# A cosFormer attention feeding a squared-ReLU MLP: the hand-written order of one Trainium2 core replaced by a list scheduler

## The chip, the cores and the metric

The kernel runs on one core of one Trainium2 chip. The metric is the device time of one launch in microseconds (us). A profile is one execution taken by the hardware profiler; its span runs from the first to the last instruction.

## The reference

There are 8 batches of 8 heads, 576 positions and a head width of 64. An attention without softmax comes first, then an MLP on all 4608 tokens:

```python
q_p = phi(q, cos_w, sin_w)      # relu(x)*cos, relu(x)*sin side by side: 128 features
k_p = phi(k, cos_w, sin_w)
kv = einsum('bhsf,bhsd->bhfd', k_p, v);  z = sum(k_p, axis=2)
x = einsum('bhsf,bhfd->bhsd', q_p, kv) / (einsum('bhsf,bhf->bhs', q_p, z) + 1e-06)
h = x.reshape(4608, 512) @ w_in          # 512 x 2048
out = relu(h)**2 @ w_out                 # 2048 x 512
```

Inputs and output are float32; the products are taken in bf16 and summed in float32.

## The kernel before

**Tiling.** Each batch's 576 positions are four tiles of 128 (j = 0 to 3) and a tail of 64 (j = 4). The attention of a batch is: features of k and q (cos half and sin half, L175 to L193), a cast of v into a tile that has a column of ones (L205), 40 small matmuls that give kv and z in one PSUM tile (`kz`, L246), its copy `kvz` (L257), the transposed features of q (by TensorE, L292, for batches 0 and 1; by a DMA transpose on SyncE's queue, L275, after that), eight matmuls of 65 columns per tile (`num`, L318), the division (three VectorE instructions, L328 to L332), and a transpose of x (TensorE L359 or DMA L350).

**First matmul** (`gemm1`, L391). A batch's 512 main tokens are two halves of 256. A slot is four of the 16 column blocks of w_in by 256 tokens: 16 matmuls of 256 columns into a two-bank PSUM tile, one ReLU of 128x1024 by ScalarE (L399), one square by VectorE (L406). The tails of two batches together are two more slots of 32 matmuls of 128 columns.

**Second matmul.** Batch 0 (L440) and one pair of tiles of batch 1 (L464) are plain, 512 columns wide. Everything else goes by pairs of 128-token tiles with Strassen's method in Winograd's form (`pair_mm`, L549): seven products (L533, eight matmuls of 256 columns each) from sums of blocks of g (`gs`, L529) and of w_out (`w2t`, L514). The products are added up by VectorE (L545) with two ScalarE copies (L569, L584), and the rows are stored from GpSimd's queue (L418).

**Order.** `slots` lists gemm1 and gemm2 slots of batch after batch; `at` and `plan` (L634 to L717) hang the attention pieces of later batches on slots by hand. All instructions of an engine run in the order in which they are issued. Loads of batches 0 to 3 are issued from GpSimd's queue, later ones from SyncE's (L709). Tiles of k, v, q and their tails have two buffers each (L62, L72). Before the slots come 31 matmuls on zeros (`warm`, L752), and batch 0's attention is written out (L771 to L790).

**PSUM.** Three pools: `hps` two tiles of two banks, `yps` two of one bank, `pa` one of two banks.

Of the kernel before, what the change touches and what calls it, by code (L numbers as in the profile page):

```python
# [15 lines left out]
FP = 512  # L16


@with_exitstack
def kernel(  # L20
# [15 lines left out]
    T = B * S  # L36
# [6 lines left out]
    assert P == 128 and H * D == 512 and D == 64 and TAIL == 64  # L43
# [4 lines left out]
    inp = ctx.enter_context(tc.tile_pool(name="inp", bufs=2))  # L48
    att = ctx.enter_context(tc.tile_pool(name="att", bufs=1))
    mlp = ctx.enter_context(tc.tile_pool(name="mlp", bufs=2))  # L50
    ps_h = ctx.enter_context(tc.tile_pool(name="ps_h", bufs=2, space=bass.MemoryType.PSUM))
    ps_y = ctx.enter_context(tc.tile_pool(name="ps_y", bufs=2, space=bass.MemoryType.PSUM))
    ps_a = ctx.enter_context(tc.tile_pool(name="ps_a", bufs=1, space=bass.MemoryType.PSUM))

    kqv = {}

    def load_main(src, nm, b, eng, parts=1):
        main = inp.tile([P, H, J, D], F32, name=nm, tag=nm, bufs=2)  # L62
        for i in range(parts):
            js = slice(i * J // parts, (i + 1) * J // parts)
            eng.dma_start(
                out=main[:, :, js, :],
                in_=src[b, :, 0:MAIN, :].rearrange("h (p j) d -> p h j d", j=J)[:, :, js, :],
            )
        kqv[nm, b] = main

    def load_tail(src, nm, b, eng):
        tail = inp.tile([P, HH, D], F32, name=nm + "t", tag=nm + "t", bufs=2)  # L72
        for g in range(2):
            eng.dma_start(
                out=tail[g * TAIL : (g + 1) * TAIL, :, :],
                in_=src[b, g * HH : (g + 1) * HH, MAIN:S, :].rearrange("h p d -> p h d"),
            )
        kqv[nm + "t", b] = tail

    def load_batch(b, eng, order):  # L80
        for nm in order:
            for part in (load_main, load_tail):
                part({"k": k, "v": v, "q": q}[nm], nm, b, eng)
# [3 lines left out]

# [28 lines left out]

# [17 lines left out]

    vexts = []
    for i in range(2):
        vx = att.tile([P, J, H, E1], BF16, name=f"vext{i}")
        vxt = att.tile([P, HH, E1], BF16, name=f"vextt{i}")
        for t in (vx, vxt):
            ones = t[:, :, :, D:E1] if t is vx else t[:, :, D:E1]  # L140
            nc.vector.memset(ones, 1.0)
        vexts.append((vx, vxt))
    kps, kvzs, kzs, qps, tqs, qpTs, xs = {}, {}, {}, {}, {}, {}, {}
    nums, xts, xtails = {}, {}, {}

    def cached(tiles, key, shape, tag, bufs):
        if key not in tiles:
            tiles[key] = att.tile(shape, BF16, name=tag, tag=tag, bufs=bufs)
        return tiles[key]


    def kp_of(b, j):
        if j == J:
            return cached(kps, (b, 1), [P, HH, F], "kpt", 1)
        return cached(kps, (b, 0), [P, J, H, F], "kp", 1)[:, j]

    def qp_of(b, j):
        if j == J:
            return cached(qps, (b, 2), [P, HH, F], "qpt", 2)
        return cached(qps, (b, j // 2), [P, 2, H, F], "qp", 2)[:, j % 2]  # L160

    def x_of(b, j):

        if j == J:
            return cached(xs, (b, 2), [P, 2, P], "xt", 2)
        return cached(xs, (b, j // 2), [P, KB, 2, P], "x", 2)[:, :, j % 2, :]

    def xT_of(b, i):
        return cached(xts, (b, i), [P, KB, 2 * P], "xT", 3)

    def xT_tails(m):

        return cached(xtails, m, [P, 2, 2, 2, TAIL], "xTt", 2)

    def feat_cos(dst, src, j):  # L175
        nc.vector.tensor_scalar(  # L176
            out=dst[:, :, 0:D],
            in0=src,
            scalar1=0.0,
            scalar2=cos_col[:, j : j + 1],  # L180
            op0=ALU.max,
            op1=ALU.mult,
        )

    def feat_sin(dst, src, j):
        nc.scalar.activation(  # L186
            out=dst[:, :, D:F], in_=src, func=ACTF.Relu, scale=sin_col[:, j : j + 1]
        )

    def feat_cos_act(dst, src, j):  # L190
        nc.scalar.activation(
            out=dst[:, :, 0:D], in_=src, func=ACTF.Relu, scale=cos_col[:, j : j + 1]
        )  # L193

    def att_k(b, j, cos=feat_cos):
        for f in (cos, feat_sin):
            f(kp_of(b, j), piece("k", b, j), j)

    def att_v(b, j, eng, h0=0, h1=H):
        copy = eng.copy if eng is nc.scalar else eng.tensor_copy  # L200
        vx, vxt = vexts[b % 2]
        if j == J:
            copy(out=vxt[:, :, 0:D], in_=piece("v", b, j))
        else:
            copy(out=vx[:, j, h0:h1, 0:D], in_=piece("v", b, j)[:, h0:h1, :])  # L205

    def warm(n):

        wm = ps_h.tile([P, 2, FP], F32, name="wm", tag="hps", bufs=2)
        for i in range(n):  # L210
            nc.tensor.matmul(
                out=wm[:, i % 2, :], lhsT=zeros[:, 0:P], rhs=zeros[:, :], start=True, stop=True
            )

    def fill(n):

        wm = ps_a.tile([P, 2, FP], F32, name="wm", tag="pa", bufs=1)
        for i in range(n):
            nc.tensor.matmul(
                out=wm[:, i % 2, :],  # L220
                lhsT=ident[:, :],
# [5 lines left out]
    def att_kv(b, part):  # L227
        vx, vxt = vexts[b % 2]
        if part == 0:
            kvzs[b] = att.tile([P, H, E1], BF16, name="kvz", tag="kvz", bufs=2)  # L230
            kzs[b] = ps_a.tile([P, 2, FP], F32, name="kz", tag="pa", bufs=1)
        kz = kzs[b]

        for j in (0, 1) if part == 0 else range(2, NS):
            for hh in range(HH):
                for half in range(2):
# [3 lines left out]
                    else:  # L243
# [3 lines left out]
                        out=kz[:, half, hh * E1 : (hh + 1) * E1],  # L247
# [5 lines left out]
        if part == 1 and b:  # L253
            att_kvz(b, nc.scalar.copy)

    def att_kvz(b, copy):
        copy(  # L257
            out=kvzs[b].rearrange("p (a h) e -> p a (h e)", a=2),
            in_=kzs[b][:, :, 0 : HH * E1],
        )  # L260

    def att_feat(b, j, parts="cs"):
        for c in parts:
            f = feat_cos if c == "c" else feat_sin
            f(qp_of(b, j), piece("q", b, j), j)

    def att_qT(b, i):

        n = 2 if i < J // 2 else 1
        nh = H if n == 2 else HH  # L270
        t = att.tile([P, n * nh, P], BF16, name="qpT", tag=f"qpT{n}", bufs=2)
        qp_of(b, 2 * i)
        src = qps[b, i]
        src = src.rearrange("p r h f -> p (r h f)") if n == 2 else src.rearrange("p h f -> p (h f)")
        nc.sync.dma_start_transpose(out=t[:, :, :], in_=src)  # L275
        for r in range(n):
            qpTs[b, 2 * i + r] = [
                t[:, r * nh + k * HH : r * nh + (k + 1) * HH, :] for k in range(nh // HH)
            ]

    def att_qT_pe(b, j, apart=False):

        nh = H if j < J else HH
        tq = ps_y.tile([P, H, P], BF16, name="tq", tag="yps", bufs=2)
        tqs[b, j] = [tq[:, 0:HH, :]]
        if apart:
            hi = ps_h.tile([P, HH, P], BF16, name="tqh", tag="hps", bufs=2)
            tqs[b, j].append(hi)
        elif nh == H:
            tqs[b, j].append(tq[:, HH:H, :])  # L290
        for h in range(nh):
            nc.tensor.transpose(  # L292
                tqs[b, j][h // HH][:, h % HH, :], qp_of(b, j)[:, h, :], ident[:, :]
            )

    def att_qT_copy(b, j, both=False):
        qpTs[b, j] = []
        for i, tq in enumerate(tqs[b, j]):
            t = att.tile([P, HH, P], BF16, name=f"qpTp{i}", tag=f"qpTp{i}", bufs=3)
            copy = nc.scalar.copy if both and i else nc.vector.tensor_copy  # L300
            copy(out=t[:, :, :], in_=tq[:, :, :])
            qpTs[b, j].append(t)

    def att_num(b, j, early=False):
        qpT, kvz = qpTs[b, j], kvzs[b]
        if early:
            num = ps_h.tile([P, 2, FP], F32, name="num", tag="hps", bufs=2)
        else:
            num = ps_a.tile([P, 2, FP], F32, name="num", tag="pa", bufs=1)
        for hh in range(HH):  # L310
            for half in range(2):
                e0 = hh * E1
                if j < J:
                    out, lhsT = num[:, half, e0 : e0 + E1], qpT[half][:, hh, :]
                else:
                    p0, p1 = half * TAIL, (half + 1) * TAIL
                    out, lhsT = num[p0:p1, 0, e0 : e0 + E1], qpT[0][:, hh, p0:p1]
                nc.tensor.matmul(  # L318
                    out=out, lhsT=lhsT, rhs=kvz[:, half * HH + hh, :], start=True, stop=True
                )  # L320
        nums[b, j] = num

    def att_div(b, j):
        n = 2 if j < J else 1
        n4 = nums[b, j][:, 0:n, 0 : HH * E1].rearrange("p b (h e) -> p b h e", e=E1)
        den = att.tile([P, 2, HH], F32, name="den", tag="den", bufs=2)
        rden = att.tile([P, 2, HH], F32, name="rden", tag="rden", bufs=2)
        nc.vector.tensor_single_scalar(  # L328
            out=den[:, 0:n], in_=n4[:, :, :, D], scalar=EPS, op=ALU.add
        )  # L330
        nc.vector.reciprocal(out=rden[:, 0:n], in_=den[:, 0:n])
        nc.vector.tensor_tensor(  # L332
            out=x_of(b, j).rearrange("p (b k) (l d) -> p b k l d", b=n, l=2),
            in0=n4[:, :, :, 0:D].rearrange("p b (k l) d -> p b k l d", l=2),
            in1=rden[:, 0:n]
            .rearrange("p b (k l) -> p b k l", l=2)
            .unsqueeze(4)
# [140 lines left out]

# [333 lines left out]
```

## Time and profile before

| what | us |
|---|---|
| time, median of 3 runs | 287.91 (287.77 to 288.2) |
| span of the profiled execution | 286.5 |
| TensorE (PE) busy, share | 279.0 (97%) |
| its weight loads (PEld) | 235.6 (82%) |
| VectorE (DVE) busy | 204.2 (71%) |
| ScalarE (ACT) busy | 161.8 (56%) |
| GpSimd (POOL) busy | 45.7 (16%) |
| moved by DMA | 53.04 MB, mean 185 GB/s |

The profiled execution's own time is not listed apart; its span stands 1.41 us below the median. A busy PE says that it never waits long, and not that each matmul takes what its columns need. Matmuls overlap, so their rate is read from the distance between starts in the chain of work or the timeline, not from a matmul's own duration. PEq, SPq and POOLq are the engines' own instruction queues.

### The profile page before, as it was taken

To read this page: it belongs to the slowest core of one execution; us is meant where nothing else is said; L and a number is where in the kernel's file an instruction comes from. 1 tells how busy PE (TensorE), PEld (TensorE's weight loads), DVE (VectorE), ACT (ScalarE), POOL (GpSimd) and SP (SyncE) were. 2 spreads that over 40 slices of the span, in tenths; PEclk is the share of its full clock that TensorE was granted. 3 is DMA by queue.
4 is the path that set the end of the run, shared out by engine and by line. 5 is a ranking of instruction groups with operands and counts; after the bars stand their busy time and mean duration, and the time that the engine had idled before them with its cause. 6 is when DMAs were issued, how large, how long until landed. Compare 5 with 4: busy or idle time off the path is not lost.

```text
span 286.5 us, 7327 instructions
## 1 busy us (share of the span) xinstructions
PE 279.0 (97%) x3067; PEld 235.6 (82%) x3067; DVE 204.2 (71%) x457; ACT 161.8 (56%) x245; POOL 45.7 (16%) x75
## 2 busy tenths in 40 slices
PE   8899999999999999999999999999999999999995
PEld 3578855888678888889988988888988888889884
DVE  1857664688697599787598776977677877547585
ACT  3764833679669669445881458844695461155210
POOL 8925507640000000000002000000000000000002
PEclk9999999999999999999999999999999999999999
DMA  7999996999457898999439975499809620300015
GB/s 236 298 206 302 329 263 197 362 364 277 57 119 187 212 275 195 237 301 212 136 106 192 348 160 165 107 267 287 227 9 237 114 46 3 140 9 2 0 76 146
DMA packets 73825, 53.04 MB, mean 185 GB/s; under 512 B 50496, under 2 KB 68416, under 8 KB 73792
## 3 DMA queue, kind: packets, MB, share of 16 engines
q1 hardware_dynamic: 63248, 26.75, 40.4%
q0 software_dynamic: 10400, 25.69, 29.8%
q8 instruction: 24, 0.39, 0.6%
q10 hardware_dynamic: 144, 0.13, 0.1%
q14 instruction: 9, 0.07, 0.1%
HBM read 36.70 MB, written 9.44 MB: 161 GB/s over the span
## 4 chain that ended last, share of the span: by engine, by line
PE 86%; DMA 5%; POOL 3%; DVE 2%; ACT 2%; issue 1%; POOLq 0%; ACTq 0%
PE hps L391 40%; PE ya L533 9%; PE yc L533 9%; PE yu L533 7%; DMA w1sb<-in_moe_w_in_dram 5%; PE yv L533 5%; PE num L318 3%; PE kz L246 3%; PE yps L464 2%; PE yps L440 2%; PE yh L440 2%; DVE ysb L545 1%; PE tq L292 1%; POOL w1sb L122 1%; DVE u L545 1%
## 5 line engine op out<-in xcount | busy, mean ns | idle before, releaser
L391 PEld LDWEIGHTS <-w1sb 128*128 128x128 bf16 x1344 | 113.4, 98 | 13.3 <-issue 2.0
L391 PE MATMUL hps<-xT,w1sb 128*128 128x256 bf16 (+1 forms) x1088 | 119.3, 266 | 1.2 <-DMA w1sb<-in_moe_w_in_dram 0.4
L399 ACT ACTIVATE rt<-hps 128x1024 bf16<-128x1024 f32 x72 | 73.7, 1023 | 68.1 <-PE hps L391 46.7
L406 DVE TENSOR_TENSOR gT<-rt 128x1024 bf16<-128x1024 bf16 x64 | 44.0, 687 | 20.1 <-ACT rt L399 20.1
L533 PEld LDWEIGHTS <-gs 128*128 128x128 bf16 x480 | 46.9, 98 | 5.4
L418 POOL DMA_DIRECT2D out_dram<-ysb x14 | 7.6, 541 | 171.6 <-DVE ysb L545 144.9
L533 PEld LDWEIGHTS <-gT 128*128 128x128 bf16 x312 | 29.8, 98 | 3.4
L332 DVE TENSOR_TENSOR x<-num,rden 128x512 bf16<-128x512 f32 x32 | 22.1, 692 | 1.1
L186 ACT ACTIVATE kp<-k,sin_col 128x512 bf16<-128x512 f32 x32 | 22.4, 717 | 0.6 <-DMA k<-in_k_dram 0.6
L186 ACT ACTIVATE qp<-q,sin_col 128x512 bf16<-128x512 f32 x32 | 22.0, 719 | 1.1 <-DMA q<-in_q_dram 1.1
L328 DVE TENSOR_SCALAR den<-num 128x8 f32<-128x8 f32 (+1 forms) x40 | 6.6, 164 | 20.6 <-PE num L318 20.4
L529 DVE TENSOR_TENSOR gs<-gT 128x1024 bf16<-128x1024 bf16 x26 | 17.8, 684 | 0.0
L533 PE MATMUL ya<-w2t,gs 128*128 128x256 bf16 x120 | 15.6, 273 | 0.0
L533 PE MATMUL yc<-w2sb,gs 128*128 128x256 bf16 x120 | 15.6, 273 | 0.0
L533 PE MATMUL yu<-w2t,gs 128*128 128x256 bf16 x120 | 15.6, 272 | 0.0
L391 PE MATMUL hps<-xTt,w1sb 128*128 128x128 bf16 x256 | 15.1, 219 | 0.2 <-ACT rt L399 0.2
L176 DVE TENSOR_SCALAR qp<-q,cos_col 128x512 bf16<-128x512 f32 x32 | 14.7, 487 | 0.0
L533 PE MATMUL yu<-w2sb,gs 128*128 128x256 bf16 x112 | 14.5, 273 | 0.0
L205 ACT CAST vext<-v 128x512 bf16<-128x512 f32 x23 | 14.1, 614 | 0.6 <-DMA v<-in_v_dram 0.6
L584 ACT COPY s<-yu 128x256 f32<-128x256 f32 x14 | 5.2, 372 | 15.6 <-PE yu L533 15.6
L176 DVE TENSOR_SCALAR kp<-k,cos_col 128x512 bf16<-128x512 f32 x21 | 10.1, 504 | 5.0 <-DMA k<-in_k_dram 5.0
L533 PE MATMUL yc<-w2sb,gT 128*128 128x256 bf16 x104 | 13.5, 273 | 0.0
(98 smaller groups left out, 340.8 us busy)
## 6 DMA issues: line engine op xcount, KB each, us to landing
out_dram<-ysb POOLq DMA_DIRECT2D x14, 512.0 KB, 4.1
k<-in_k_dram SPq DMA_DIRECT2D x5, 1024.0 KB, 7.9
v<-in_v_dram POOLq DMA_DIRECT2D x4, 1024.0 KB, 8.6
v<-in_v_dram SPq DMA_DIRECT2D x4, 1024.0 KB, 8.7
q<-in_q_dram SPq DMA_DIRECT2D x4, 1024.0 KB, 6.7
q<-in_q_dram POOLq DMA_DIRECT2D x3, 1024.0 KB, 12.7
k<-in_k_dram POOLq DMA_DIRECT2D x3, 1024.0 KB, 10.0
w1sb<-in_moe_w_in_dram POOLq DMA_DIRECT2D x4, 512.0 KB, 11.2
```

The costliest lines, as they stand in the source:

```text
L176: nc.vector.tensor_scalar(out=dst[:, :, 0:D], in0=src, scalar1=0.0, scalar2=cos_col[:, j : j + 1], op0=ALU.max, op1=ALU.mult,)
L186: nc.scalar.activation(out=dst[:, :, D:F], in_=src, func=ACTF.Relu, scale=sin_col[:, j : j + 1])
L205: copy(out=vx[:, j, h0:h1, 0:D], in_=piece("v", b, j)[:, h0:h1, :])
L246: nc.tensor.matmul(out=kz[:, half, hh * E1 : (hh + 1) * E1], lhsT=lhsT, rhs=rhs, start=(j == 0 and hh == 0), stop=(j == J and hh == HH - 1),)
L318: nc.tensor.matmul(out=out, lhsT=lhsT, rhs=kvz[:, half * HH + hh, :], start=True, stop=True)
L332: nc.vector.tensor_tensor(out=x_of(b, j).rearrange("p (b k) (l d) -> p b k l d", b=n, l=2), in0=n4[:, :, :, 0:D].rearrange("p b (k l) d -> ...
L391: nc.tensor.matmul(out=out, lhsT=w1sb[:, kb, hb * P : (hb + 1) * P], rhs=rhs, start=(kb == 0), stop=(kb == KB - 1),)
L399: nc.scalar.activation(out=rt[:, :, :], in_=hps[:, :, :], func=ACTF.Relu)
L406: nc.vector.tensor_tensor(out=dst, in0=rt[:, :, :], in1=rt[:, :, :], op=ALU.mult)
L440: nc.tensor.matmul(out=ypss[b][tt], lhsT=gTs[b][:, hb, tt * P : (tt + 1) * P], rhs=w2sb[:, hb, :], start=(hb == 0), stop=(hb == HB - 1),)
L529: nc.vector.tensor_tensor(out=t[:, :, :], in0=in0, in1=in1, op=op)
L533: nc.tensor.matmul(out=acc, lhsT=lhs[:, hb, :], rhs=rhs[:, hb, :], start=(hb == 0), stop=(hb == HB2 - 1),)
```

## The change

The kernel's order is no longer written by hand. A class `Plan` takes every step with its engine, an estimated duration, the keys it reads and writes, and a due time; a greedy pass puts at each moment the ready step with the earliest due time on the engine that is free first, and the steps are then issued in that order. What is issued by hand as before: the loads of batch 0, of w_in, of batch 1 and of w_out, and batch 0's attention up to x of its first two tiles.

```diff
+class Plan:
+    LAG = {"PE": 0.24, "ACT": 0.1, "DVE": 0.1, "POOL": 0.1, "SP": 0.1}
+    def add(self, eng, dur, fn, r=(), w=(), due=None, size=0.0, lag=None, name="", after=0.0):
...
+        at = max([self.given.get(key, 0.0) for key in (*r, *w)] + [after])
...
+    def order(self, t0, rate, fixed):
...
+        free = {"PE": t0, "ACT": t0, "DVE": t0, "POOL": t0, "SP": t0, "DMA": t0}
...
+            i = min((i for i in waiting[e] if ready[i] <= s + 0.02), key=lambda i: (due[i], i))
...
+            if size:
+                free["DMA"] = max(free["DMA"], end) + size / rate
+                end = free["DMA"] + fixed
...
+    T0 = 16.8
...
+    plan.given.update({("v", j): 41.0 for j in range(J)})
+    plan.given.update({("kt", 0): 37.0, ("vt", 0): 42.0, ("qt", 1): 31.5, ("qt", 0): 26.0})
...
+        plan.run(T0, 0.38, 2.0)
```

Loads have one buffer per input (two for the tails of q), and all loads of batches 2 to 7 are steps of the plan on GpSimd's queue:

```diff
-        main = inp.tile([P, H, J, D], F32, name=nm, tag=nm, bufs=2)
+        main = home(inp, [P, H, J, D], nm, dtype=F32)
...
+    TAILS = {"k": 1, "v": 1, "q": 2}
...
+    def plan_load(b, nm, due, eng="POOL"):
+        size = 1.05
+        add(eng, 0.95, lambda: load_main(nm, b, ENG[eng]), w=[(nm, j) for j in range(J)], due=due, size=size)
```

The first matmul of batches 1 to 7 runs over all 512 main tokens at once; the tails of the eight batches (8 x 64 = 512 tokens) are a ninth batch. PSUM is six single banks and one double one (`abank`, for `kz` and `num`); a unit is four matmuls of 512 columns into bank 2, 0 or 1, with its own ReLU of 128x512; four units share one square of 128x2048. Batch 0 keeps its two halves.

```diff
+    def unit_mm(m, hb, to):
...
+        for kb in range(KB):
+            nc.tensor.matmul(
+                out=out_,
+                lhsT=w1sb[:, kb, hb * P : (hb + 1) * P],
+                rhs=x_block(m, kb),
+                start=(kb == 0),
+                stop=(kb == KB - 1),
+            )
```

The second matmul: batch 0 is plain as before; batches 1 to 8 each have seven products of two halves (eight matmuls of 256 columns each) over blocks of 256 tokens. Sums of products are kept in PSUM: where a sum goes on in another bank, ScalarE copies the bank (a seed), and later products are added on top by the matmuls.

```diff
+    YA, YB, YC = 3, 4, 5
...
+        prod(1)
+        seed(YA, YB)
+        prod(2)
+        last(YA, 0, 0, False)
+        prod(5)
+        add("ACT", cost("ACT", 512, "psum"), lambda: nc.scalar.copy(out=five_of(m)[:, :, :], in_=half_bank(YC)),
+            r=[("bank", YC)], w=[("five",)])
+        prod(6)
+        seed(YB, YC)
+        prod(7)
+        prod(3)
+        last(YB, 0, 1, True)
+        store(0)
+        last(YC, 1, 1, True)
+        prod(4)
+        last(YC, 1, 0, False)
+        store(1)
```

`last` is a ScalarE copy to the output tile, or with the flag a VectorE addition of product 5. Stores are issued from SyncE's queue; the ninth batch's are two groups of four of 64 rows. All cos features are made by VectorE and all sin features by ScalarE.

The built order of the changed kernel, engine by engine, has these places that the prediction speaks of. GpSimd: the four w_out loads end the part by hand, then `qt` of batch 2 (two tails), `q`, `k`, and later `v` of batch 2. ScalarE: sin features of batch 1's k and its tail, sin of batch 2's q tail, sin of batch 1's q tail, casts of v of batch 1 (tiles 2, 3, tail), four sin features of batch 2's q, copy `kvz` of batch 1. VectorE: cos of batch 1's k, square, cos of batch 2's q tail, cos of batch 1's q tail, casts of v of batch 1 (tiles 0, 1). TensorE: transposed q features of batch 1's tiles 2 and 3, the second matmul of batch 0 (16 steps of four matmuls), and in it, after the fifth step, `kz` of batch 1 in three parts, `num` and the transposes of x of batch 1.

## The prediction

> **What bounds the kernel now.** I read the page's busy times first, then the chain of work in order of time, then the timeline of the first 50 us. PE is busy 279.0 of 286.5 us, and the chain is PE nearly throughout, so every us is either a matmul's columns or a wait of PE.
>
> ```profile
> PE 279.0 (97%) x3067; PEld 235.6 (82%) x3067; DVE 204.2 (71%) x457; ACT 161.8 (56%) x245; POOL 45.7 (16%) x75
> PEclk9999999999999999999999999999999999999999
> ```
>
> The chain's stretches give PE's rates (start, us, what):
>
> ```profile
> 77.31 1.73 PE yps L464 x8
> ...
> 81.25 0.87 PE ya L533 x8
> ...
> 128.81 8.92 PE hps L391 x112
> ...
> 143.85 0.49 PE kz L246 x16
> ```
>
> 512 columns cost 1.73/8 = 216 ns and 256 columns 109 ns; the 112 are 48 wide ones (48 x 0.1092 = 5.24) and 64 of 128 columns, so (8.92 - 5.24)/64 = 57.5 ns; a 65-column one costs 0.030. Wide matmuls are hardly cheaper per column (216 against 2 x 109), so the change can save little on PE; the question is its waits. Where they come from is in the timeline (start, us, engine, line, what, idle before it):
>
> ```profile
> 16.79 1.96 PE L391 MATMUL hps<-xT,w1sb 128*128 128x128 bf16 x32
> ...
> 33.87 0.75 POOL L129 DMA_DIRECT2D w2sb<-in_moe_w_out_dram  x1 [2.48 <-DMA k<-in_k_dram]
> ...
> 34.61 0.91 POOL L65 DMA_DIRECT2D q<-in_q_dram  x1
> ...
> 39.15 1.44 DVE L205 CAST vext<-v 128x512 bf16<-128x512 f32 x4 [0.81 <-DMA v<-in_v_dram]
> ...
> 42.21 1.13 PE L246 MATMUL kz<-vext,kp 128*128 128x65 bf16 x32
> ```
>
> The reader is to see that loads arrive late here: GpSimd issues the last w_out load at 33.87 because it waits for one of the transfers under way, v of batch 1 lands only at 39.15, and PE comes to `kz` after that, at 42.21. DMA is full to 44 us. A small load on this queue stands behind the large ones (issues between 30 and 50 us, KB each, us to landing; the q tails of that answer were issued at 44.9, when the queue had drained):
>
> ```profile
> vt<-in_v_dram POOLq DMA_DIRECT2D x3, 64.0 KB, 7.7
> qt<-in_q_dram POOLq DMA_DIRECT2D x2, 64.0 KB, 2.4
> ```
>
> **The sum on PE.** After the first real matmul at 16.79, before has 960 of 256 and 384 of 128 columns in the first product (104.8 + 22.0), 96 of 512 and 840 of 256 in the second (20.8 + 91.7), 584 small ones (17.6) and 84 transposes (4.8): 261.7. After has 512 of 512, 96 of 256 and 64 of 128 (110.7 + 10.5 + 3.7), 64 of 512 and 896 of 256 (13.8 + 97.8), the same 584, and 72 transposes (4.1): 258.3. **Minus 3.4 us**: 1.7 of it from tails at 512 columns, the rest from widths and transposes. Before's last matmul ends at 283.09 (282.05 + 1.04), so 283.09 - 16.79 - 261.7 = 4.6 us are waits: 1.9 up to the first Strassen product at 81.25 (its place in the sum is 62.6 after the start), 2.7 after it.
>
> **Up to 16.79** nothing changes: the loads and batch 0's attention are issued as before. The q load of batch 1 has now to wait for the features of batch 0's q (the last cos ends at 17.04; it was issued at 12.71), but it stands behind w_in, whose last quarter is waited for at 24.43; I take no loss, at most the 4.3 us by which it is issued later.
>
> **16.8 to 36.5: +1.1.** w_in's third and fourth quarters are waited for as before (0.3 and 0.4). All four q tiles of batch 1 are transposed before the second matmul starts, not three. The fourth needs ScalarE's sin, which stands behind the two ReLUs of the last half slot: that slot ends near 34.4, two times 0.59 and 0.72 later it is 35.9. The second matmul starts at 36.5; by the sum it would be 35.4 (before: 34.9, then 0.5 lost at 35.94).
>
> **The main wait: +3.9.** In the built order both VectorE and ScalarE have a feature of batch 2's q tail ahead of the v casts of batch 1. That tail load is issued after the last w_out load, so not before 34.6, behind v and three quarters of w_out; with 7.7 us for such a load it lands at 42.3, and since q, issued at 34.61, lands with the draining of the queue near 45, I take 43.0 (ends: 37.0, by the 2.4 of an empty queue, and 45.3). The two tails (0.35 each) and two casts (0.42 each) make 44.65 before `kz` can start; PE is there, 4.3 us after 36.5, at 40.8. PE runs in order, so all later work slips. Then ScalarE has four sin features of batch 2's q (4 x 0.72 from 46.0, when that q lands) ahead of the `kvz` copy (0.59): `num` waits **+1.1**. At the end of this stage `num` of tile 3 is followed directly by the transposes of its x: a copy of 0.69 on VectorE and the division (0.17 + 0.20 + 0.69) stand between: **+1.8** with the smaller waits. In before these stretches had other work between them.
>
> **Steady state: waits as before, 2.7, and 1.5 on the way in.** ScalarE gains work: 144 ReLUs at 0.59 (row of a 128x512 PSUM copy, 586 ns) for 72 at 1.02 are +10.5, and 40 PSUM copies at 0.59 for 29 at 0.37 are +12.9, so about 185 us. A window of 28.5 us (one first and one second product) has 16 x 0.59 + 5 x 0.59 + 8 x 0.72 + 2 x 0.50 + 1.6 + 0.6 = 21.4 on it. VectorE loses about 25 (additions of products 42 to 11, +5 cos, small ones). Both stay below PE; that hides them, and a ReLU has two units (1.7 us) until its bank is wanted. A seed from PSUM to PSUM is in no row: between 0.37 (128x256) and 0.69 (VectorE, 128x512 float32); I take 0.59, nearest in shape. In the first such window VectorE has the eight sums of w_out (5.5) besides, and three features (0.5 + 0.4 + 0.7) stand ahead of the first seed: +1.5. Below these, 0; above, x's transposes: their DMA lands a median 4.0 after its issue and is wanted about 9 us after the last `num` of a batch, behind a transpose of q (3.9): it may cost 1 us in each of four windows.
>
> **The end: +1.6 and +1.9.** The ninth batch's products have no first matmul beside them. The first waits for ReLU and square (2.2 after the last unit against 1.75 of products: 0.5), product 7 for the seed (0.2 + 0.6 + 0.1, nothing else ready), product 4 for 0.1. After the last matmul come a ScalarE copy (0.59 for 0.42) and, on one queue, the rest of eight stores of 64 rows, about 0.55 apart: 3 x 0.55 more than before. 3.4 us (286.5 - 283.1) become 5.3.
>
> **Sum.** 44.65, plus the rest of the stream (258.3 less 22.2 up to `kz`: 236.1), plus 1.1 + 1.8 + 1.5 + 2.7 + 1.6, plus 5.3: a span of 294.7. The median stands 1.41 above the span: **296.1 us**, 2.9% slower.
>
> **A rule that would make it longer.** At the start the 31 matmuls on zeros take 8.46 us where 31 x 0.216 would be 6.7, so a cold PE lost 1.75 though the page grants it full clock. The Trainium skill, "TensorE: Matmul & The Clock Gate", section "Part 1: The HAM clock gate", says that PE falls to half clock after an idle window of some 3.4 us and needs as much busy time to recover. No wait of before is long enough to show it. If PE's wait at `kz` (3.9 us) sets this off, the price by the row is 1.75 again.
>
> **Rivals.** (1) The tail load lands at 45.3 (+2.3), or the wait slows PE (+1.75), or both: 297.8 to 300.1. For: DMA at its limit to 44 us. (2) The tail load lands before the casts are due (37.0): their chain then starts at 39.15, `kz` is hardly late, and 3.9 is not paid: 292.2; with 1.1 and 1.8 gone as well, 289.3. Against: the 7.7 us row. (3) Transposes or single-buffered loads arrive late in each window: 4 us more, 300.1. (4) Faster: the price is PE's own waits. If the new order removes the 1.9 and 2.7 of before and adds only the end's 3.5 less the sum's 3.4, it is 287.9 + 0.1 - 4.6 = 283.4; it turns faster once all of PE's waits ahead of the end stay below 4.5 us. For: no engine but PE is full in steady state. Against: the in-order queues above. That the change does not do what it says (waits elsewhere unchanged, PE sum unmoved) would give 287.9 + 3.5 = 291.4; I count it with (2).
>
> **Chances.** Forecast (293 to 297.5) 0.45; (1) 0.17; (2) 0.17; (3) 0.09; (4) 0.09; between (2) and no change 0.03. Range: from 288.5 to 300.5, which leaves out (4) and the far end of (3). A difference under 0.2% (0.6 us) can't be told from none: faster 0.09, same 0.03, slower 0.88.
>
> **What would show it.** Right: a gap of PE of some 4 us before `kz` of batch 1 near 41 to 45, with VectorE and ScalarE idle on a q-tail load before it; PE's sum near 258 after 16.8; a gap near 1 us before product 7 at the end and over 5 us after the last matmul. Wrong: the v casts at 39; PE gaps in each window; a second matmul that starts at 35; or a PE rate other than 216 ns.

## The result, and the profile after

The changed kernel takes **334.08 us** (median of 4 runs, 333.01 to 338.89) against 288.06 (287.77 to 289.03): a ratio of **1.159, 95% interval 1.154 to 1.163**. One of the four runs, the one of 338.89, counts as slow and is not in the ratio. The forecast of 296.1 had the sign right and missed the size by 38 us, and the time lies far above the range. The profiled execution has a span of 331.2 us, 36.5 over the forecast's 294.7.

The page of the changed kernel, with the rows that answer to those shown of before, and the shares of the chain of work:

```profile
PE 286.7 (87%) x2403; PEld 187.3 (57%) x2407; DVE 183.8 (55%) x368; ACT 173.6 (52%) x305; POOL 60.1 (18%) x89
...
PEclk9999979966999996898967999999999999999998
...
PE 58%; DMA 32%; DVE 3%; ACT 2%; issue 2%; POOL 1%; ACTq 0%; POOLq 0%; DVEq 0%
```

PE is 58% of the chain where it was 86% before; a third is DMA now, and the granted clock dips several times. The clock row's digits are the 40th parts of the span, 8.3 us each: all dips but the last digit lie in the first 22, before 183 us. The table by stage says the same in us (window; its length; PE, PEld, DVE, ACT, POOL busy; granted clock; DMA share; GB/s). Before:

```profile
16.00:60.00 44.00, 43.31 (x474) 32.71 (x472) 27.31 (x65) 23.53 (x34) 20.36 (x28) 1.00 1.05 284
60.00:120.00 60.00, 59.50 (x710) 49.98 (x709) 49.11 (x116) 45.14 (x73) 3.34 (x6) 1.00 0.84 206
120.00:180.00 60.00, 59.90 (x676) 53.80 (x674) 45.31 (x98) 36.13 (x54) 3.77 (x7) 1.00 0.76 200
```

After:

```profile
16.00:60.00 44.00, 36.42 (x372) 25.81 (x374) 25.62 (x59) 26.55 (x48) 22.24 (x30) 0.96 1.15 284
60.00:120.00 60.00, 49.09 (x432) 29.07 (x431) 44.37 (x95) 38.45 (x71) 14.73 (x21) 0.91 0.97 214
120.00:180.00 60.00, 43.95 (x339) 26.57 (x338) 28.64 (x59) 27.99 (x52) 8.86 (x13) 0.83 1.15 196
180.00:330.00 150.00, 143.44 (x1153) 98.43 (x1151) 76.26 (x128) 71.06 (x122) 2.97 (x5) 1.00 0.30 80
```

From 16 to 180 us PE stands 34.5 us idle (7.6 + 10.9 + 16.0) where before it stood 1.3, and part of its busy time ran at less than full clock. After 180 us, when nearly all loads are in, PE is busy almost throughout, at clock 1.00. So the new order can run without waits; something before 180 us prevents it, and the DMA engines are fuller there (0.97 and 1.15 against 0.84 and 0.76) though they move hardly more bytes per us (214 and 196 GB/s against 206 and 200). What PE's neighbours wait for (waiting instruction and what ended the wait; us in total, times, longest):

```profile
DVE qp L270 <- DMA qpT<-qp: 25.7, 3, 12.6
...
ACT qp L268 <- DMA qpT<-qp: 20.6, 4, 9.0
```

A feature of the next batch's q (L268, L270) overwrites the tile that the query transpose (L333, a DMA on SP) still reads. VectorE and ScalarE run in order, so ReLUs and squares behind it wait too, and PE behind those. The two largest waits of PE before 80 us, in its timeline:

```profile
46.23 1.04 PE L311 MATMUL abank<-vext,kp 128*128 128x65 bf16 x16 [5.86 <-DVE vext L288]
...
63.10 2.75 PE L435 MATMUL bank<-xT,w1sb 128*128 128x512 bf16 x12
74.75 1.86 PE L435 MATMUL bank<-xT,w1sb 128*128 128x512 bf16 x4 [8.89 <-ACT rt L448]
```

The first is the wait at `kz` that the prediction named. The second it did not have, and SP's own timeline shows its cause:

```profile
48.91 22.53 SPq L333 DMA_TRANSPOSE qpT<-qp  x2
```

Two transposes hold SP for 22.5 us, while POOL's queue has four 1 MB loads of batches 2 and 3 under way (issued from 47.62 to 57.67). Later waits of PE behind transposes are 7.6 us (to 130.9, for a transpose of x, which stands on SP's queue among those of q), 3.0 (to 146.3) and 3.3 (to 169.0) behind query transposes, and 1.2 for x again. Over the whole run the query transposes land a median 8.4 us after their issue, where before it was 3.9; those of x land after 4.3 (before: 4.0). In the kernel before, loads of batches 4 to 7 stood in one row with the transposes on SP; now all loads but the first are on POOL's queue, beside them.

### The profile page after: what moved, and what is told of

It reads as the page before. It is cut to its first block, busy times and chain, and to the rows that moved or that the text cites. A ratio compares the mean times of both kernels' runs of the same rounds, so it can differ in the third digit from the quotient of the medians.

```text
span 331.2 us, 6047 instructions
## 1 busy us (share of the span) xinstructions
PE 286.7 (87%) x2403; PEld 187.3 (57%) x2407; DVE 183.8 (55%) x368; ACT 173.6 (52%) x305; POOL 60.1 (18%) x89
## 3 DMA queue, kind: packets, MB, share of 16 engines
q1 hardware_dynamic: 48272, 21.50, 36.5%
q0 software_dynamic: 12032, 31.46, 34.5%
## 4 chain that ended last, share of the span: by engine, by line
PE 58%; DMA 32%; DVE 3%; ACT 2%; issue 2%; POOL 1%; ACTq 0%; POOLq 0%; DVEq 0%
PE bank L435 29%; PE bank L587 24%; DMA qpT<-qp 17%; DMA q<-in_q_dram 5%; DMA v<-in_v_dram 4%; DMA k<-in_k_dram 3%; DMA qt<-in_q_dram 2%; PE abank L364 2%; PE abank L311 1%; DMA xT<-x 1%; DVE x L384 1%; DVE kp L270 1%; ACT rt L448 0%; ACT qp L268 0%; PE bank L292 0%
## 5 line engine op out<-in xcount | busy, mean ns | idle before, releaser
L435 PE MATMUL bank<-xT,w1sb 128*128 128x512 bf16 x512 | 132.7, 395 | 20.6 <-ACT rt L448 11.9
L448 ACT ACTIVATE rt<-bank 128x512 bf16<-128x512 f32 x128 | 75.9, 597 | 76.3 <-PE bank L435 76.0
L435 PEld LDWEIGHTS <-w1sb 128*128 128x128 bf16 x512 | 49.5, 101 | 66.4 <-issue 21.1
L460 DVE TENSOR_TENSOR gT<-rt 128x2048 bf16<-128x2048 bf16 x32 | 39.1, 1222 | 44.4 <-ACT rt L448 44.3
L587 PEld LDWEIGHTS <-gT 128*128 128x128 bf16 x512 | 49.8, 99 | 20.5 <-DVE gT L460 3.6
L587 PE MATMUL bank<-w2sb,gT 128*128 128x256 bf16 x384 | 51.3, 277 | 4.7 <-DVE gT L460 3.3
L587 PE MATMUL bank<-w2t,gs 128*128 128x256 bf16 x256 | 34.0, 277 | 0.0
L268 ACT ACTIVATE qp<-q,sin_col 128x512 bf16<-128x512 f32 x32 | 21.8, 714 | 21.7 <-DMA qpT<-qp 20.6
L270 DVE TENSOR_SCALAR qp<-q,cos_col 128x512 bf16<-128x512 f32 x32 | 14.9, 510 | 31.5 <-DMA qpT<-qp 25.7
L268 ACT ACTIVATE kp<-k,sin_col 128x512 bf16<-128x512 f32 x32 | 21.3, 715 | 1.7 <-PE abank L311 1.1
L384 DVE TENSOR_TENSOR x<-abank,rden 128x512 bf16<-128x512 f32 x31 | 21.4, 691 | 1.1
L270 DVE TENSOR_SCALAR kp<-k,cos_col 128x512 bf16<-128x512 f32 x32 | 14.8, 506 | 9.0 <-DMA k<-in_k_dram 5.8
L780 ACT COPY ysb<-bank 128x512 f32<-128x512 f32 x16 | 9.4, 585 | 16.7 <-PE bank L587 16.5
L776 DVE TENSOR_TENSOR ysb<-bank,y 128x512 f32<-128x512 f32 x16 | 11.0, 688 | 12.8 <-issue 7.7
L587 PE MATMUL bank<-w2sb,gs 128*128 128x256 bf16 x128 | 16.6, 273 | 0.0
L587 PE MATMUL bank<-w2t,gT 128*128 128x256 bf16 x128 | 16.3, 273 | 0.0
```

The source lines that it names most:

```text
L268: eng.activation(out=dst[:, :, lo : lo + D], in_=src, func=ACTF.Relu, scale=col)
L270: eng.tensor_scalar(out=dst[:, :, lo : lo + D], in0=src, scalar1=0.0, scalar2=col, op0=ALU.max, op1=ALU.mult,)
L384: nc.vector.tensor_tensor(out=x[:, a:z], in0=n4[:, :, :, 0:D].rearrange("p b (k l) d -> p b k l d", l=2), in1=rden[:, a:z] .rearrange("p b ...
L435: nc.tensor.matmul(out=out_, lhsT=w1sb[:, kb, hb * P : (hb + 1) * P], rhs=x_block(m, kb), start=(kb == 0), stop=(kb == KB - 1),)
L448: eng.activation(out=rt_of(m, u)[:, i, :], in_=bank[to][:, :], func=ACTF.Relu)
L460: nc.vector.tensor_tensor(out=dst, in0=rt, in1=rt, op=ALU.mult)
```

## The experiments

**Theory A**: a query transpose that shares the DMA engines with loads of another queue takes several times as long, and the in-order engines carry this to PE. **B**: the planned order itself, with its single buffers, makes the waits. **C**: the falling clock is most of it. A fourth reading came with the first runs: the DMA is simply too full before 180 us, from whatever queue. The times below are single runs beside one or more of the kernel before (287.6 to 288.7) unless an interval is given; four runs of one version (e14) spread over 2.4 us, so a difference of 1 or 2 us between single runs settles nothing. The first number is the time, the span is that of the profiled execution.

**e1.** In `att_qT` the main transposes are left out; what reads them finds zeros.

```diff
-        nc.sync.dma_start_transpose(out=t[:, :, :], in_=src)
+        if n == 1:
+            nc.sync.dma_start_transpose(out=t[:, :, :], in_=src)
```

> Leaves out the twelve main transposes of the query features (SP, L333, batches 2 to 7); the numerators of these batches read a tile filled with zeros once at the start, and every other instruction and its order stay. Theory A (a transpose that shares the DMA engines with loads from POOL's queue takes 8 to 17 us instead of 2, and the features of the next batch, in order ahead of the ReLUs, wait for it): the waits of PE around 63, 123, 146 and 165 us shrink to under 2 us each (8.9 + 7.6 + 4 + 4.2 of idle, some 5 us of slow clock behind them), the wait at 46.2 stays, span 298 to 304 against 331.2. Theory B (the planned order itself: features and casts of later batches ahead of the ReLUs, single input buffers, a load queue blocked at its head; the transposes only happen to end last): other waits take their place, span above 315. Theory C (the falling clock is the larger part and follows any wait): the first wait alone costs most, span above 318.

299.97 us, span **297.8**. The wait at `kz` stays (4.7 us), and behind it PE waits at most 1.4 us at a time, as the windows show:

```profile
60.00:120.00 60.00, 57.78 (x533) 35.69 (x532) 53.93 (x115) 46.64 (x86) 17.99 (x25) 1.00 0.77 217
120.00:180.00 60.00, 60.00 (x536) 40.78 (x535) 41.62 (x84) 41.80 (x76) 9.77 (x14) 1.00 0.75 174
```

B and C in their strong forms fall: order and first wait are unchanged, and 33.4 us are gone with twelve transposes.

**e2.** `for i in range(parts if b < 4 else 0)` in `load_main`.

> Leaves out the twelve 1 MB loads of batches 4 to 7 (their features are made from the inputs of batch 3 again); the small loads of the tails, all transposes and the order stay. Theory A: the waits before 90 us stay (those loads are of batches 2 and 3), those at 123, 146 and 165 go, 7.6 + 4 + 4.2 us and some 4 of slow clock: span 308 to 314; each transpose of the queries after 90 us issues in 2 to 3 us. Rival (the transposes are slow by themselves, or through the stores and the small loads beside them): they still take 5 to 12 us and the span stays above 325.

314.54 us, span 312.6, within theory A's range. After 87 us the query transposes issue in 1.7 to 3.0 us and PE has no wait of 1 us or more; the wait before 80 us is there, and longer (13.5). So a transpose is not slow by itself: it needs the loads beside it.

**e3, e4.** `plan_load(b, nm, None, "POOL" if b < 4 else "SP")`, and `"SP"` for all.

> The loads of batches 4 to 7 are issued by SP, in one row with the transposes, as the kernel before did; the planner knows it and puts them in by its due times. Theory A in its narrow form (what hurts is the loads of a second queue beside the transposes): transposes after 90 us issue in 2 to 4 us as in the kernel before, span 308 to 316. Rival (bytes: the DMA engines are 90 to 99% busy to 176 us, and the same bytes early cost the same from any queue): span 327 to 335. Rival (a load that waits for its buffer now holds up the transposes behind it on SP): span above 335.

> As the run before, with the loads of batches 2 and 3 on SP too. Theory A in its narrow form: the wait at 63 to 75 us goes as well, span 296 to 304. Rival of bytes: 325 to 335. Rival of the row on SP: the first loads stand behind each other's buffers and ahead of the first transposes, so the wait at 46 us grows by the 5 us that a load takes to issue and land, span above 330.

e3: 327.37, span 325.6; e4: 310.46, span **308.4**. e3 misses its forecast: after 90 us the transposes are mostly down (1.8 to 6.9 us), but the pair at 49 us, still beside POOL's loads, took 25.5 and PE's wait there 16.7 (another of 4.7 came at 166), which gave most of the gain back. Why this wait was 8.9, 13.5 and 16.7 us in three kernels whose loads differ only from batch 4 on stays open. e4 removes it, and neither reading is enough: 23 us come with the queue and the order in which a load then stands among the transposes, against the reading of bytes, but 4 to 12 remain over the forecast, with the DMA share at 1.03 from 60 to 120 us.

**e5.** The loads stay on POOL, each batch behind a small copy that reads the transposes' result.

```diff
+            add("POOL", 0.1, lambda i=i: nc.gpsimd.tensor_copy(out=gate_to[:, i : i + 1], in_=homes["qpT", i][:, 0, 0:1]),
+                r=[("qpT", "main", i)], w=[("gate",)])
...
+        add(eng, 0.95, lambda: load_main(nm, b, ENG[eng]), r=[("gate",)], w=[(nm, j) for j in range(J)], due=due, size=size)
```

> Loads stay on POOL's queue, but those of batch b (3 to 7) stand behind two copies of one column from the tiles that the query transposes of batch b-1 write, so they are not issued before these transposes have landed. Theory A by time (what hurts is a load under way beside a transpose, not the queue's kind): the two transposes at 49 us are done by about 60, not 73, the wait of 8.9 us at 63 to 75 us falls below 4, those at 123, 146 and 165 us below 3 each, span 300 to 314. Rival (the held loads land too late, and the features wait for them in the same place): waits of DVE and ScalarE for q move up from 5.8 us to over 12, span above 322.

310.55, span 308.4. PE's waits after 60 us are at most 1.4 us. The pair at 53 us still took 10.1, and the wait at `kz` grew to 8.2, so part of the gain is lost there. Same queue, other times: what matters is that loads and transposes don't meet.

**e6, e7.** Two start values in the planner's model, with loads on POOL (e6) and on SP (e7).

```diff
-        free = {"PE": t0, "ACT": t0, "DVE": t0, "POOL": t0, "SP": t0, "DMA": t0}
+        free = {"PE": t0, "ACT": t0, "DVE": t0, "POOL": 34.0, "SP": t0, "DMA": 43.0}
```

> Loads on POOL as in the changed kernel; only two start values of the planner's model change: POOL free at 34.0 and the DMA at 43.0 us, where the trace shows them free, in place of 16.8. By the prediction's main step (the tail feature of batch 2 stands ahead of the casts for batch 1 because the planner took its load for early): the wait of PE at 46.2 us falls from 5.9 to under 3. Theory A: the waits for the query transposes stay, span 322 to 332. Theory C (the first wait sets off the others): span under 318.

> All loads of batches 2 to 7 on SP and the planner's start values of the run beside it. If the two faults add up, the waits that the kernel with all loads on SP kept before 60 us (2.1 and 4.6 us, some 2 of slow clock) halve: span 301 to 306 against 308.4. If its remaining waits are the DMA's and not the plan's, 306 to 311.

e6 is the prediction's main step by itself. The products of `kz` (count; ns min/median/max; first and last start) of the changed kernel between 36 and 60 us, and of e6:

```profile
L311 PE MATMUL abank<-vext,kp x32: 191/232/262, 46.2 to 49.3; 128*128 128x65 bf16 x32
```

```profile
L311 PE MATMUL abank<-vext,kp x48: 191/193/198, 40.2 to 57.7; 128*128 128x65 bf16 x48
```

`kz` starts at 40.2, without a wait; the prediction had put PE there at 40.8 if nothing were late. And the time is 334.21, span 332.3, just over the end of theory A's range: the six us were given back later. The pair at 50.6 took 20.1 us and PE waited 3.3 behind it; then it waited 4.6 and 4.4 at 101 and 109 (behind a load of v and a transpose of x) and 8.7 at 164, behind a tail load of q that took 17.4 to land. e7: 309.75, span 307.9, its second branch. C falls for good here: without the first wait the others come all the same.

**e8, e9.** The kernel before, its loads of batches 4 to 7 moved from SP to POOL (e8) or ScalarE (e9).

```diff
-        at(34 if b == 4 else second[b - 3] + 6, load_batch, b, nc.sync, "kv")
+        at(34 if b == 4 else second[b - 3] + 6, load_batch, b, nc.gpsimd, "kv")
...
+        at(first[b - 2] + 5, load_batch, b, nc.gpsimd, "q")
```

> The kernel before, with the loads of batches 4 to 7 on POOL's queue (behind its stores) in place of SP. Theory A with no help from the new order: its transposes after 90 us take 5 to 12 us and PE waits for them, 292 to 306 us against 288. Rival (the old order has the slack: what is transposed is needed a window later; so the fault needs the new order as well): within 1 us of 288, though the transposes are as slow.

> The kernel before with the loads of batches 4 to 7 issued by ScalarE, so from a second hardware queue beside SP's transposes, in the same places of the program where POOL issued them in the run that took 363.8 us. If any second queue beside a transpose slows it: the pair of query transposes after 120 us takes 15 to 25 us again and the time is 330 to 365 us. If only POOL's software queue does: the pair takes 4 to 7 us and the time is 289 to 300 us (ScalarE loses some 20 us of its 125 idle ones to issuing). Third: ScalarE waits for the buffers ahead of its ReLUs and PE stands behind them although the transposes are quick, 300 to 330.

e8: **363.83 us**, span 362.1, far above its forecast of 292 to 306; one changed queue costs 75 us in an order that was full. The order and the bytes are those of before, so neither the plan (B) nor the fullness of the DMA by itself can be the cause here. PE's four longest waits after 100 us, 4.3, 21.6, 12.2 and 26.3 us, are all for query transposes; the second of them in PE's timeline:

```profile
149.47 0.62 PE L318 MATMUL num<-kvz,qpT 128*128 128x65 bf16 x8 [21.64 <-DMA qpT<-qp]
```

SP's timeline of before, of e8 and of e9 (two main transposes of q each):

```profile
115.77 3.79 SPq L275 DMA_TRANSPOSE qpT<-qp  x2
```

```profile
123.28 24.12 SPq L275 DMA_TRANSPOSE qpT<-qp  x2
```

```profile
123.33 9.01 SPq L275 DMA_TRANSPOSE qpT<-qp  x2
```

e9: 315.0, span 313.2, between its branches: a second hardware queue lengthens the pair too, to 9.0 us, POOL's software queue to 24.1. In e9 12.1 us of PE's waits are for transposes; two more (5.5 and 3.2) are for ScalarE, part of its third branch.

**e10.** `plan_load(b, nm, None, "ACT")`.

> The changed kernel with the loads of batches 2 to 7 issued by ScalarE; the planner counts their issue times on it. Same question in the new order: any second queue, transposes of 8 to 20 us after 48 us and a span of 325 to 345; only POOL's queue, transposes of 2 to 6 us and a span of 305 to 320.

303.07, span 301.3, better than either branch: most query transposes take 1.8 to 4.6 us, and the pair of batch 2 6.5.

**e11, e15, e16.** Loads of batch b not planned before 12 us ahead of the window of its attention: with SP and the true start values (e11), on POOL (e15), and with the old start values (e16).

```diff
+    def plan_load(b, nm, due, eng="POOL", after=0.0):
...
+            plan_load(b, nm, None, "SP", win[b - 2][0] - 12 if b >= 3 else 0.0)
```

> All loads on SP, the planner's start values as the trace shows them, and the loads of batch b (3 to 7) not before 12 us ahead of the window in which its attention is planned, so that less DMA work is crowded into the time before 180 us (DMA share 1.0 to 1.09 in the kernel with the loads on SP, 0.76 to 0.84 in the kernel before). If crowding is what is left of the loss: share under 0.95 from 80 us on, span 294 to 303. If what is left are latencies in the order: 304 to 312.

> The kernel that spread its loads (296.5 us with them on SP), with the same spread plan and the loads on POOL. POOL waits only for buffers there, so nothing in the run itself holds a load back until the transposes have gone. If the queue beside the transposes is what costs: transposes of 8 to 20 us again, span 312 to 335. If the spread alone does it: 296 to 302.

> The spread loads on SP, with the planner's start values as in the changed kernel (POOL and DMA free at 16.8 us). If the prediction's main step (tail feature of batch 2 ahead of the casts, 3.9 us) is worth what it said: the wait at the kz products is back with 2 to 5 us and the span is 2 to 5 us above 296.5. If order repairs it on SP: within 1.5 us of 296.5.

e11: 298.45, span **296.5**; its windows:

```profile
16.00:60.00 44.00, 38.93 (x415) 27.52 (x414) 26.95 (x65) 27.94 (x50) 9.43 (x13) 1.00 1.16 264
60.00:120.00 60.00, 54.67 (x495) 33.90 (x494) 46.68 (x96) 40.17 (x75) 0.00 (x0) 1.00 0.94 226
120.00:180.00 60.00, 60.00 (x537) 40.57 (x536) 40.60 (x85) 41.32 (x74) 0.00 (x0) 1.00 0.91 246
```

The clock is 1.00 up to 180 us and 34.7 us of the loss are gone, with the work unchanged. e15: 303.35, span 301.6: its first pair still takes 18.1 us (PE waits 5.6), but after 75 us, when loads and transposes come at different times, the others take 1.5 to 4.0 on the same queue. On POOL the spread takes 30.7 us off e6 (332.3 to 301.6), where the queue alone took 24.4 (e7); its branch "spread alone" is right. e16: 303.97, span 301.9: the start values are worth 5.4 us here, a little over the branch of 2 to 5. The wait at `kz` is 1.4 us; the larger one comes right behind it, for the copy `kvz`, which stands behind the sin features of batch 2's q:

```profile
53.35 0.60 PE L364 MATMUL abank<-kvz,qpTp 128*128 128x65 bf16 x8 [6.14 <-ACT kvz L322]
```

**e12, e13, e14, e17.** As e11, with four blocks of batch 2 transposed on PE (`plan_qT_pe`). In e12 to e14 part of the computation is changed: batch 1's second multiplication lacks its seeds in banks 4 and 5 (and in e12 one block uses another's transposes; the last section has the reasoning); e17 has bank 3 alone.

> As the run beside it, with the eight heads' transposes of batch 2's four main blocks on PE and copied by VectorE (1.8 us more PE, 2.8 us more VectorE), because the DMA is full to 80 us whatever the order. If the two main transposes of batch 2 hold up the start: 3 to 6 us faster than the run beside it. If not: 1 to 2 us slower by its own work.

> As the run with batch 2's transposes on PE, with the fourth block transposed only after the first block's numerators (in that run the planner let it take the first block's copy, so one block of batch 2 used the wrong transposes). The instructions are the same in number: span 293 to 296 against 294.1.

> The run beside it, and the eight last stores (of the ninth batch) issued by POOL (four), SP (two) and ScalarE (two) in place of SP alone. In the changed kernel they leave SP one after the other from 323.1 to 328.1 us, and the span ends 3.1 us later. If this issuing carries the term of the end: 1.8 to 2.6 us less, span 291 to 293.5, time 292.5 to 295. If the landing of the last store or PE carries it: within 0.5 us of the run beside it.

> The version of the mended block order, with the transposes of batch 2 all in bank 3 (which the second product's first product overwrites) and not in banks 3 to 5 (in the three kernels with banks 4 and 5 the seeds of batch 1's second multiplication, copied there afterwards, went missing from the sums). One bank in place of three makes each transpose wait for the copy before it: 0 to 2 us over the 293.1 us span of the run with three banks, time 294 to 298 and still slower than the kernel before; a time under 288 would need the 5 us of waits before 60 us to go, which this does not touch.

Spans 294.1, 293.1, 293.8 and 294.6; e14 takes 294.86 us, ratio 1.0225 (1.0178 to 1.0273); e17, with nothing left out, **295.71 us, ratio 1.0255 (1.0202 to 1.0308)**. e12 is 2.4 us faster than e11, between its branches (3 to 6 faster, or 1 to 2 slower); e13 and e17 are as forecast. e14 is a miss: from the last copy to the end of the span it took 6.5 us (e13: 6.2), though the last issue ended 1.8 us after that copy and not 3.3; the landing on ScalarE's queue (median 4.7 us, on SP's 2.4 in e13) probably took it; no run separates the two. No version came under the kernel before.

## Why the prediction was wrong, step by step

**The step that failed** is "Steady state: waits as before, 2.7", with the cover it gave for the transposes: a landing of 4.0 us, wanted 9 us later. That 4.0 was x's; the query transposes (3.9) were counted only as what stands ahead of x's, and no term said that the next features, in order ahead of the ReLUs, wait for them. Both figures were measured where transposes and later loads share SP's row and follow each other. The change moves the loads of batches 4 to 7 to POOL's queue and lets the planner start them as soon as a buffer is free. I had counted no cost for a load that changes its queue, nor for what it meets there. What the runs show in its place is a pair of query transposes that holds SP for 22.5 us beside POOL's loads, with 8.9 us of PE's idle time behind it. Rival (3), "transposes late in each window", was the right mechanism and was priced at 4 us; it was about 29 with its clock (331.2 - 301.9, the span of e16, where only the queue and the times of the loads differ). The price of a DMA was taken from a row with other neighbours than it has after the change.

**The ledger.** From 16 us to the end e11 and the changed kernel differ by 24.5 us of PE's idle time (280.5 - 262.7 = 17.8 against 315.2 - 272.9 = 42.3) and by 10.2 of busy time (272.9 - 262.7) for the same matmuls: the first are waits, the second the clock. Together they are 34.7; by e16, 29.3 of them go with the loads' queue and times, the other 5.4 with the start values.

**The clock.** In 72 to 80 us, the end of the wait of 8.9 us and what follows it, the granted clock is 0.52 (columns as above):

```profile
64.00:72.00 8.00, 1.86 (x9) 0.75 (x8) 0.11 (x1) 0.10 (x1) 0.00 (x0) 0.84 1.06 231
72.00:80.00 8.00, 5.25 (x22) 1.80 (x22) 5.58 (x11) 5.40 (x10) 1.94 (x3) 0.52 0.54 183
```

In narrower windows the changed kernel's clock is 0.50 in five stretches of 3.4, 10.2, 6.8, 3.4 and 10.2 us (from 45.5, 69.4, 127.4, 147.9 and 168.4), whole multiples of some 3.4. PE is busy for 22.1 us in them, and half of that, 11.1, answers to the 10.2. Each begins in a wait of PE of 3.0 us or more, or within 2 us of its end; no shorter wait by itself brings one. The rule of the Trainium skill that the prediction cited ("TensorE: Matmul & The Clock Gate", section "Part 1: The HAM clock gate") agrees with the half clock and with the 3.4 us, though waits of 3.0 and 3.3 us, a little under its window, were enough here. I gave it one possible wait, and it acted on five: 10.2 us, not 1.75.

**Right.** *PE's sum.* Before has 265.5 us of busy PE after 16 us, e11 262.7: -2.8 where -3.4 was said. *The second matmul* starts at 35.88 (36.5 said). *The wait at `kz`*: place and cause as said (VectorE and ScalarE idle for the tail of q to 45.22 and 45.10), size 5.9 for 3.9, since the tail landed at the late end of its range, 45.1 for 43.0; e6 shows it by taking it away. *Product 7* waits 0.71 us for its seed ("near 1"). **Size off:** the end took 7.0 us after the last matmul, for 5.3. The last matmul ends at 324.2; the copy is done at 324.8, and the stores of the ninth batch leave SP to 328.1 and land after that. In e14 quicker issuing from three queues did not buy it back.

**The small terms and the rivals.** In e11, where they can be read without the large loss, PE waits 1.14, 1.39 and 0.82 us for x's transposes and copy at 51 to 58 us (1.8 said), 1.93 for a ReLU at 70 and 0.66 for the first seed at 80 (1.5 said), and 1.24 and 0.78 for the DMA of x. Of rival (1) both halves came, the late tail and the slow clock; they are not what made the size. Rivals (2) and (4) are out: no wait went away. Of the 4.6 us that the prediction called waits of before, only 1.6 are idle time in the windows (5.0 after 16 us, less 3.4 of the end); the rest is busy time above the sum, so there was less to win than rival (4) had it. In the prediction's 44.65, the terms named add up to 44.54, and 296.1 is 2.8% over 287.91, not 2.9%; neither changes anything. ScalarE came to 173.6 us of busy time where about 185 was said, VectorE to 183.8 where about 179 was (204.2 less 25).

**The forecast without the failed step.** e16 keeps loads and transposes apart and leaves the rest of the changed kernel as it is. Its span is 301.9, still 7.2 over the forecast's 294.7: PE waits 1.4 us for `kz` and 6.1 for `kvz` where 3.9 and 1.1 were said (2.5 more), the clock falls behind that wait (2.1 us more busy time than e11), and the end takes 7.2 for 5.3; the remainder is smaller terms. So the step that failed is most of the miss and not all of it. e11 comes nearer to the forecast, 296.5, but partly by luck: with its start values the main wait, 3.9 of the forecast, is all but absent (0.2 us at `kz`). It is 10.0 us over before: 2.8 less of PE, 12.8 more idle (17.8 against 5.0), where the prediction had -3.4 and +11.6. It also shows where the intended gain is: 2.8 us on PE against 3.3 us of end and 9.5 of waits, nearly all ahead of 120 us, so that even the best versions stay 2 to 3% behind.

## What to carry over

When a change moves a transfer to another queue, list what else is under way there at that time and price the urgent transfer with that neighbour, not with the row it had alone: here 3.8 us became 24.1. Keep loads that are not urgent off the engines while a DMA transpose is awaited, by one row of issue, by a release time in the planner or by a wait on the transpose. A list scheduler that models the DMA as one line of work at a fixed rate does not see this, and starting everything as early as buffers allow makes it worse (332.3 us of span in e6, 301.6 in e15, on the same queue).

## What was not expected of the hardware

DMA transposes beside POOL's loads took longer than both would one after the other, by an estimate. In e8 from 121.8 to 150 us PE is idle for 21.6 us and little goes on but one pair of transposes, 3 MB of loads with their tails, and stores (queue: packets, MB, share of 16 engines' time):

```profile
q0 software_dynamic: 1283, 4.53, 61.0%
q1 hardware_dynamic: 2891, 0.73, 48.8%
```

The same queue of the kernel before, 115 to 122 us, with the transposes first in the row and no loads but those behind them:

```profile
q1 hardware_dynamic: 4678, 1.18, 76.0%
```

One packet took 0.488 x 16 x 28.2 / 2891 = 0.076 us there and 0.76 x 16 x 7 / 4678 = 0.018 here. The two shares in e8 add up to more than 100%, so a packet's time contains waiting. The loads suffer as well: v and q of batch 5 land 21.5 and 22.1 us after their issue (8.7 and 6.7 are the medians on SP in the kernel before). The Trainium skill, "DMA: Bandwidth & Descriptors", section "🔬 Queues, rings and completion order", says that an engine serves its rows in turn, a packet at a time. Sharing in turn agrees with these rows as far as it goes, but 4.53 MB at the 300 GB/s that the page of before often shows are 15 us, and 5 more for the pair and the tail's transpose (3.8 + 1.3 in the kernel before) would be 20, not 28; where the rest goes stays open. The section "🎯 Rules for kernel authors" of the same page of the Trainium skill says, where it speaks of transposes that corrupt each other, that a transpose next to ordinary DMAs needs nothing. That is about right results; in time, these runs show, such neighbours can cost much.

The seeds lost in e12 to e14 fit "PSUM — Partial Sum Buffer" of the Trainium skill, section "🔬 PSUM: the matmul accumulator": by that page of the Trainium skill a matmul that opens a sum clears the written marks of its whole bank, only TensorE sets them, and a later product overwrites what is not marked. The transposes opened sums in banks 4 and 5 eight times each, and by the same rule ScalarE's copies set no mark; with bank 3 alone (e17) nothing is lost. The marks themselves are in no trace.
